# Chunked attention, then a two-layer leaky network: Q's copies on ScalarE, whole-tile exponentials, and a new written order

## The chip, the cores and the metric

The kernel runs on one core of one Trainium2 chip. The metric is the device time of one execution in microseconds (us), and the number compared is the median over several executions. The core's engines work side by side, each through its own list of instructions in order, and wait for each other through semaphores. The profile's names are: PE (TensorE matmuls), PEld (TensorE weight loads), DVE (VectorE), ACT (ScalarE), POOL (GpSimd) and SP (SyncE, here only a queue of DMAs).

## What is computed

Inputs are q, k and v of shape (8, 8, 576, 64), and two weight matrices of 512 x 2048 and 2048 x 512, all float32. The output is 4608 x 512, float32.

```python
q_c, k_c, v_c = (t.reshape(B, H, nc, 64, D) for t in (q, k, v))      # chunks of 64 positions
scores = q_c @ k_c.T / sqrt(D)
scores = scores - max(scores, axis=-1)
attn = exp(scores);  attn = attn / (sum(attn, axis=-1) + 1e-9)
out = attn @ v_c
x = out.transpose(0, 2, 1, 3).reshape(4608, 512)
h = x @ w_in
y = maximum(0.01 * h, h) @ w_out
```

## The kernel before

**Attention.** The tokens are cut into 36 units `u` of 128 positions (two chunks, all eight heads). For a unit, Q and K are loaded as 16-bit floats by POOL's DMA queue (`g`), and turned so that the head dimension lies on the partitions: for early units by TensorE transposes (`tq`, `tk`), from unit 14 on by transposing DMAs on SP's queue (`tdq`, `tdk`; lines 560 and 566), which land in tiles `QT` and `KT`. Q then goes into one of three standing tiles `QZ` whose other half is zero, by two copies of 64 partitions each (`cq`, line 573). `s` makes eight small matmuls, which give the scores `Sp` (one PSUM bank for all units) of 128 rows x 8 groups x 64.

**Softmax.** Two ways stand side by side. In the first, `m` takes the row maximum (line 591, DVE), `b` subtracts it from the whole score tile (line 596, DVE, in place in PSUM from unit 9 on), `x` makes one exponential of the whole tile (line 628, ACT), and `z` sums the rows (638), adds the tiny constant (640, tile `ze`) and takes the reciprocal (642), all on DVE. In the second, which the units 14, 16, 18, ... 34 use (eleven of the 36), `nb` multiplies the maximum by the negative scale (line 605, DVE, 128 x 8), and `f` makes eight exponentials of 64 columns each, with `nb` as bias, and lets ACT sum the rows on the way (line 613); `z` then leaves out its row sum. After either, `n` normalises (line 648; on POOL from unit 10 on), a transposing DMA turns the result (`d`, line 671, SP's queue), `v` multiplies with V, and `a` copies the attention output into `xT` on ACT (line 705).

**Network.** The tokens are worked in blocks `j`: two of 128 tokens, then 17 of 256. From block 2 on the second layer, and from block 9 on the first too, is done by seven half-size products in place of eight, which need sums and differences of the operands. First layer: `M` (line 321) up to block 8, with `G` (line 335, ACT) as leaky evacuation; from block 9 on `V` (line 418), with evacuations `lx` (ACT, line 449), `la` (DVE, line 455, adds a kept half) and `lp` (leaky, ACT, line 437), and sums `xs` of the input (line 389, POOL for most blocks). Second layer: `sum` makes the operand sums `SG` (line 205; the fourth of each of the blocks 8 to 15 is on POOL, the others on DVE), `R` the products (line 229), and `comb` the evacuations (ACT, lines 262 and 281, tiles `keep` and `osb`; DVE, line 283) and the store by SP's queue.

**What sets the order.** All of this is emitted by one written-out string, `ORDER`: a list of stage names with arguments, walked from left to right. Each stage issues its instructions at that point, so each engine's list, and SP's and POOL's queues, are in the order of the string. PSUM banks of the `m` kind are given out by a second string, `BANKS`, in the same walk. Nothing is reordered afterwards; a waiting instruction holds up all behind it on its engine.

```python
        nc.vector.tensor_copy(out=QZ[u % NQZ][part, :, :, s, :], in_=QT[u][part])           # stage_cq
        (nc.gpsimd if u >= UP else nc.vector).tensor_tensor(                                # stage_n
        (nc.gpsimd if (j, n) in SG_POOL else nc.vector).tensor_tensor(out=SG[j, n], in0=x, in1=y, op=op)
        (nc.gpsimd if j in XS_POOL else nc.vector).tensor_tensor(out=s[:, n - 1], in0=x, in1=y, op=op)
```

Of the kernel before, what the change touches and what calls it, by code (L numbers as in the profile page):

```python
# [8 lines left out]
FP16 = mybir.dt.float16  # L9
FP32 = mybir.dt.float32  # L10
# [6 lines left out]
def kernel(  # L17
# [52 lines left out]
    def need(*what):  # L70
        assert what in made, what
# [69 lines left out]
    minus = sbp.tile([128, 8], FP32, name="minus")  # L141
    nc.vector.memset(minus, -SCL)
# [427 lines left out]
    def stage_cq(u, s):  # L570
        made.add(("dq", u, s))
        part = slice(s * CH, (s + 1) * CH)
        nc.vector.tensor_copy(out=QZ[u % NQZ][part, :, :, s, :], in_=QT[u][part])
# [26 lines left out]
    Z: dict[int, bass.AP] = {}  # L600
    NB: dict[int, bass.AP] = {}

    def stage_nb(u):
        NB[u] = sbp.tile([128, 8], FP32, name="nb", tag="nb", bufs=2)
        nc.vector.tensor_tensor(out=NB[u], in0=MX.pop(u), in1=minus, op=ALU.mult)  # L605

    def stage_f(u, i0, i1):

        if i0 == 0:
            E[u] = sbp.tile([128, 8, CH], FP16, name="ex", tag="ex", bufs=2)  # L610
            Z[u] = sbp.tile([128, 8], FP32, name="z", tag="z", bufs=2)
        for i in range(i0, i1):
            nc.scalar.activation(  # L613
                out=E[u][:, i, :],
                in_=SP[u][:, i, :],
                func=AFT.Exp,
                bias=NB[u][:, i:i + 1],
                scale=SCL,
                accum_out=Z[u][:, i:i + 1],
            )  # L620
        made.add(("f", u, i0))
        if i1 == 8:
            need("f", u, 0)
            del SP[u], NB[u]

# [6 lines left out]
    def stage_z(u):  # L632
        if u in Z:
            need("f", u, 4)
            z = Z.pop(u)
        else:
            z = sbp.tile([128, 8], FP32, name="z", tag="z", bufs=2)
            nc.vector.tensor_reduce(out=z, in_=E[u], axis=AXL.X, op=ALU.add)
        ze = sbp.tile([128, 8], FP32, name="ze", tag="ze", bufs=2)
        nc.vector.tensor_tensor(out=ze, in0=z, in1=tiny, op=ALU.add)  # L640
        ZI[u] = sbp.tile([128, 8], FP32, name="zi", tag="zi", bufs=2)
        nc.vector.reciprocal(out=ZI[u], in_=ze)  # L642
# [107 lines left out]
    def zero_act(i):  # L750
# [151 lines left out]
```

## Time and profile before

| what | value |
|---|---|
| time, median of 3 runs | 281.63 us (279.67 to 282.55) |
| profiled execution, its own time | 281.67 us |
| span of the profile in that execution | 279.9 us |
| busy PE / PEld | 267.9 us / 243.7 us |
| busy DVE / ACT / POOL | 231.2 us / 202.3 us / 165.2 us |
| mean granted TensorE clock | 0.994 |

The span runs from the first instruction of the program to the last; the 1.8 us between it and the execution's own time lie outside the profile. Busy shares are averages over a start-up (about 18 us, until the first layer begins), a long middle part and a tail; what a wait costs is read where it stands.

### The profile page before, as it was taken

To read this page: it belongs to the slowest core of one execution; us is meant where nothing else is said; L and a number is where in the kernel's file an instruction comes from. 1 tells how busy PE (TensorE), PEld (TensorE's weight loads), DVE (VectorE), ACT (ScalarE), POOL (GpSimd) and SP (SyncE) were. 2 spreads that over 40 slices of the span, in tenths; PEclk is the share of its full clock that TensorE was granted. 3 is DMA by queue.
4 is the path that set the end of the run, shared out by engine and by line. 5 is a ranking of instruction groups with operands and counts; after the bars stand their busy time and mean duration, and the time that the engine had idled before them with its cause. 6 is when DMAs were issued, how large, how long until landed. Compare 5 with 4: busy or idle time off the path is not lost.

```text
span 279.9 us, 9161 instructions
## 1 busy us (share of the span) xinstructions
PE 267.9 (96%) x3705; PEld 243.7 (87%) x3705; DVE 231.2 (83%) x461; ACT 202.3 (72%) x531; POOL 165.2 (59%) x190
## 2 busy tenths in 40 slices
PE   7879999999999999999899897999999999999994
PEld 4569967999999999999898896999998999999994
DVE  7875679999987759888789999989999888587773
ACT  5656644675757775766797887989897997867661
POOL 8838646970374181968689666798979456003000
PEclk9979999999999999999999999999999999999999
DMA  9999999999699999999999969499999905020213
GB/s 149 139 187 183 206 178 156 155 145 125 115 131 159 206 187 200 139 165 164 200 101 201 165 124 105 115 132 127 175 178 151 158 15 115 4 94 2 78 40 112
DMA packets 159242, 38.35 MB, mean 137 GB/s; under 512 B 150240, under 2 KB 154720, under 8 KB 159200
## 3 DMA queue, kind: packets, MB, share of 16 engines
q0 software_dynamic: 111392, 18.10, 95.1%
q1 hardware_dynamic: 46768, 19.41, 37.5%
q8 instruction: 29, 0.48, 0.7%
q10 hardware_dynamic: 1040, 0.26, 0.4%
q14 instruction: 13, 0.11, 0.1%
HBM read 36.70 MB, written 9.44 MB: 165 GB/s over the span
## 4 chain that ended last, share of the span: by engine, by line
PE 74%; DVE 12%; ACT 4%; DMA 3%; POOL 3%; issue 2%; DVEq 0%; ACTq 0%; POOLq 0%
PE hT L321 19%; PE prX L229 17%; PE xbank L418 10%; PE xpr L418 7%; PE pr L229 6%; PE prZ L229 4%; DMA w_inT<-in_moe_w_in_dram 3%; DVE ze L640 3%; PE prW L229 2%; PE oP L464 2%; PE Sp L582 2%; PE xp L684 2%; DVE SG L205 2%; DVE xkeep L455 2%; ACT ex L613 2%
## 5 line engine op out<-in xcount | busy, mean ns | idle before, releaser
L321 PE MATMUL hT<-xT,w_inT 128*128 128x128 f16 (+1 forms) x768 | 63.7, 240 | 0.2 <-DMA w_inT<-in_moe_w_in_dram 0.2
L229 PEld LDWEIGHTS <-SG 128*128 128x128 f16 x544 | 51.0, 98 | 7.5 <-issue 1.9
L648 POOL TENSOR_TENSOR en<-ex,zi 128x512 f16<-128x512 f16 x26 | 28.0, 1077 | 49.9 <-DVE zi L642 15.9
L321 PEld LDWEIGHTS <-w_inT 128*128 128x128 f16 x768 | 54.7, 99 | 2.9 <-issue 0.2
L455 DVE TENSOR_TENSOR xkeep<-xpr,xkeep 128x512 f32<-128x512 f32 x60 | 39.3, 682 | 10.1 <-ACT xkeep L449 7.4
L335 ACT ACTIVATE gT<-hT 128x512 f16<-128x512 f32 x64 | 36.5, 603 | 11.4 <-PE hT L321 11.2
L449 ACT ACTIVATE xkeep<-xbank 128x512 f32<-128x512 f32 x60 | 36.1, 625 | 6.8 <-PE xbank L418 6.5
L229 PEld LDWEIGHTS <-gT 128*128 128x128 f16 x400 | 37.3, 98 | 4.3 <-ACT gT L437 0.3
L418 PEld LDWEIGHTS <-WS 128*128 128x128 f16 x640 | 38.2, 98 | 1.4 <-DVE xkeep L455 0.8
L437 ACT ACTIVATE gT<-xkeep 128x512 f16<-128x512 f32 x56 | 33.7, 661 | 6.2 <-DVE xkeep L455 6.2
L91 POOL DMA_DIRECT2D k_in<-in_k_dram x39 | 32.7, 841 | 9.0 <-DMA VB<-in_v_dram 5.3
L91 POOL DMA_DIRECT2D q_in<-in_q_dram x39 | 33.5, 865 | 5.6 <-DMA w_outT<-in_moe_w_out_dram 2.6
L229 PE MATMUL prX<-TW,SG 128*128 128x256 f16 x272 | 35.3, 273 | 0.2 <-DVE SG L205 0.2
L262 ACT ACTIVATE keep<-prX 128x256 f32<-128x256 f32 x51 | 20.4, 401 | 20.7 <-PE prX L229 19.3
L418 PEld LDWEIGHTS <-w_inT 128*128 128x128 f16 x480 | 29.1, 98 | 1.8 <-issue 1.1
L591 DVE TENSOR_REDUCE mx<-Sp 128x8 f32<-128x512 f32 x36 | 24.5, 682 | 6.5 <-PE Sp L582 6.0
L205 DVE TENSOR_TENSOR SG<-gT 128x1024 f16<-128x1024 f16 x34 | 24.5, 720 | 3.8 <-ACT gT L335 3.5
L613 ACT ACTIVATE ex<-Sp,nb 128x64 f16<-128x64 f32 x88 | 26.3, 331 | 1.8 <-DVE nb L605 1.7
L705 ACT ACTIVATE xT<-xp 128x512 f16<-128x512 f32 x36 | 22.2, 617 | 6.4 <-PE xp L684 6.3
L98 POOL DMA_DIRECT2D VB<-in_v_dram x24 | 23.3, 978 | 4.0 <-PE xp L684 4.0
L418 PE MATMUL xbank<-xs,WS 128*128 128x128 f16 x320 | 22.9, 219 | 0.0
L205 POOL TENSOR_TENSOR SG<-gT,SG 128x1024 f16<-128x1024 f16 x8 | 17.3, 2167 | 9.1 <-DVE SG L205 4.2
(96 smaller groups left out, 510.3 us busy)
## 6 DMA issues: line engine op xcount, KB each, us to landing
out_dram<-osb SPq DMA_DIRECT2D x35, 256.0 KB, 3.1
q_in<-in_q_dram POOLq DMA_DIRECT2D x31, 128.0 KB, 5.9
k_in<-in_k_dram POOLq DMA_DIRECT2D x31, 128.0 KB, 6.8
VB<-in_v_dram POOLq DMA_DIRECT2D x8, 288.0 KB, 7.4
VB<-in_v_dram POOLq DMA_DIRECT2D x16, 144.0 KB, 4.7
w_inT<-in_moe_w_in_dram POOLq DMA_DIRECT2D x8, 256.0 KB, 7.7
w_outT<-in_moe_w_out_dram POOLq DMA_DIRECT2D x4, 512.0 KB, 11.1
q_in<-in_q_dram POOLq DMA_DIRECT2D x8, 64.0 KB, 6.4
```

Of the source, the lines that this page charges most:

```text
L91: nc.gpsimd.dma_start(out=to, in_=rows)
L205: (nc.gpsimd if (j, n) in SG_POOL else nc.vector).tensor_tensor(out=SG[j, n], in0=x, in1=y, op=op)
L229: nc.tensor.matmul(out=to[:, i, :], lhsT=left[:, f, i * 128:(i + 1) * 128], rhs=right[:, f, :], start=(j, where) not in opened, stop=(f == ...
L321: nc.tensor.matmul(out=hT[:, i, :], lhsT=w_inT[:, t, fc * 128:(fc + 1) * 128], rhs=xT[:, t, r0:r0 + tb], start=(t == 0), stop=(t == NT - 1),)
L335: nc.scalar.activation(out=gT[j][:, nf * a:nf * a + nf, c0:c0 + tb], in_=HT.pop((j, a, p)), func=AFT.Prelu, bias=0.0, scale=1.0, alpha=0.01,)
L418: nc.tensor.matmul(out=to[:, i, :], lhsT=left[:, t, i * 128:(i + 1) * 128], rhs=right[:, t], start=(n in (1, 2, 5) and t == 0 and i == 0), ...
L437: nc.scalar.activation(out=gT[j][:, f0:f0 + 4, hi * 128:hi * 128 + 128], in_=of, func=AFT.Prelu, bias=0.0, scale=1.0, alpha=0.01)
L449: nc.scalar.activation(out=XK[j, s, n], in_=XB[j, s], func=AFT.Copy, bias=0.0, scale=1.0)
L455: nc.vector.tensor_tensor(out=to, in0=of, in1=to, op=ALU.add)
L591: nc.vector.tensor_reduce(out=MX[u], in_=SP[u], axis=AXL.X, op=ALU.max)
L613: nc.scalar.activation(out=E[u][:, i, :], in_=SP[u][:, i, :], func=AFT.Exp, bias=NB[u][:, i:i + 1], scale=SCL, accum_out=Z[u][:, i:i + 1],)
L648: (nc.gpsimd if u >= UP else nc.vector).tensor_tensor(out=E[u], in0=ex, in1=ZI.pop(u).unsqueeze(2).to_broadcast((128, 8, CH)), op=ALU.mult)
```

## The change

Three things are changed together.

1. `stage_cq` gets a flag, and all 44 copies of Q into `QZ` that take a transposed DMA's result now carry it: they are ACTIVATE copies on ACT, and no longer copies on DVE.
2. `nb` and `f` are gone. All 36 units take the maximum off with `b` on DVE, make one exponential of 128 x 512 with `x` on ACT, and sum the rows in `z` on DVE. A constant tile (`minus`) and its memset go with them.
3. `ORDER` is written anew from end to end. The stages and the products in it are the same apart from 1 and 2, and `BANKS`, `LOADS`, the number of filler matmuls and the assignment of sums to POOL stay.

```diff
-    minus = sbp.tile([128, 8], FP32, name="minus")
-    nc.vector.memset(minus, -SCL)
...
-    def stage_cq(u, s):
+    def stage_cq(u, s, act=0):
         made.add(("dq", u, s))
         part = slice(s * CH, (s + 1) * CH)
-        nc.vector.tensor_copy(out=QZ[u % NQZ][part, :, :, s, :], in_=QT[u][part])
+        to = QZ[u % NQZ][part, :, :, s, :]
+        if act:
+            nc.scalar.activation(out=to, in_=QT[u][part], func=AFT.Copy, bias=0.0, scale=1.0)
+        else:
+            nc.vector.tensor_copy(out=to, in_=QT[u][part])
...
-    def stage_nb(u):
-        NB[u] = sbp.tile([128, 8], FP32, name="nb", tag="nb", bufs=2)
-        nc.vector.tensor_tensor(out=NB[u], in0=MX.pop(u), in1=minus, op=ALU.mult)
...
-        for i in range(i0, i1):
-            nc.scalar.activation(
-                out=E[u][:, i, :],
-                in_=SP[u][:, i, :],
-                func=AFT.Exp,
-                bias=NB[u][:, i:i + 1],
-                scale=SCL,
-                accum_out=Z[u][:, i:i + 1],
-            )
...
     def stage_z(u):
-        if u in Z:
-            need("f", u, 4)
-            z = Z.pop(u)
-        else:
-            z = sbp.tile([128, 8], FP32, name="z", tag="z", bufs=2)
-            nc.vector.tensor_reduce(out=z, in_=E[u], axis=AXL.X, op=ALU.add)
+        z = sbp.tile([128, 8], FP32, name="z", tag="z", bufs=2)
+        nc.vector.tensor_reduce(out=z, in_=E[u], axis=AXL.X, op=ALU.add)
...
     ORDER = (
-        "R7.3.0 tdq23 d18 cq23.1 d19 tdk22 tdq24 f20.0.4 f20.4.8 z20 comb7.3 comb7.4 G8.6.0 G8.7.0 tdk23 G8.5.0 V9.0.1 "
...
-        "lx11.1.1 comb10.1 cq26.0 cq27.1 cq25.0 comb9.3 d23 sum10.2 z24 vl6.0 xs11.4 sum10.4 g30 n24 V11.0.2 V11.1.2 "
...
+        "d18 st640 tdk23 x20 cq22.1.1 G8.6.0 cq22.0.1 z20 comb7.3 comb7.4 G8.5.0 G8.7.0 cq23.1.1 st512 d19 V9.0.1 s21 "
...
+        "x24 tdk27 comb9.4 lp10.0.1.0 comb9.3 la10.1.3 z24 V11.0.1 V11.1.1 v22 s25 R10.1.0 lp10.1.1.1 lp10.1.1.0 "
+        "cq27.0.1 lx11.0.1 lx11.1.1 a22 comb10.1 sum10.2 vl6.0 sum10.4 g30 xs11.4 n24 V11.0.2 V11.1.2 R10.2.0 la11.0.2 "
```

Three places show what the new order does.

**VectorE at the entry of block 9**, where the unit 20 is in its softmax and the last sums of the block 7 are evacuated (`mx` the maximum, `Sp` the scores, `QZ` the tiles of Q, `osb` the output rows, `ze` and `zi` the row sum and its reciprocal, `SG` operand sums of the second layer). Before:

```order
L591 TENSOR_REDUCE mx<-Sp 128x8
L605 TENSOR_TENSOR nb<-mx,minus 128x8
L573 COPY QZ_66<-QT 64x8x64
L283 TENSOR_TENSOR osb_2722<-prZ,keep 128x256
L573 COPY QZ_67<-QT 64x8x64
L640 TENSOR_TENSOR ze<-z,tiny 128x8
L642 RECIPROCAL zi<-ze 128x8
L283 TENSOR_TENSOR osb_2618<-prZ,keep 128x256
L205 TENSOR_TENSOR SG<-gT 128x1024
```

And of the changed kernel, whose line numbers are lower by 2 to 28:

```order
L593 TENSOR_REDUCE mx<-Sp 128x8
L598 TENSOR_TENSOR Sp<-Sp,mx 128x512
L281 TENSOR_TENSOR osb_2697<-prZ,keep 128x256
L610 TENSOR_REDUCE z<-ex 128x8
L612 TENSOR_TENSOR ze<-z,tiny 128x8
L614 RECIPROCAL zi<-ze 128x8
L281 TENSOR_TENSOR osb_2634<-prZ,keep 128x256
L203 TENSOR_TENSOR SG<-gT 128x1024
```

The multiplication `nb` and two copies have left this stretch; a subtraction over the whole tile and a row sum have come in.

**ScalarE at the same place**, from the exponentials of the unit 20 to the first evacuations of the block 9 (`gT` the hidden layer, `xkeep` a kept quarter of the first layer). Before:

```order
L613 ACTIVATE ex,z<-Sp,nb 128x64 x8
L281 ACTIVATE osb_2722<-prX 128x256
L335 ACTIVATE gT<-hT 128x512 x3
L449 ACTIVATE xkeep<-xbank 128x512 x2
L262 ACTIVATE keep<-prX 128x256
```

And of the changed kernel:

```order
L604 ACTIVATE ex<-Sp 128x512
L573 ACTIVATE QZ_66<-QT 64x8x64
L333 ACTIVATE gT<-hT 128x512
L573 ACTIVATE QZ_66<-QT 64x8x64
L279 ACTIVATE osb_2697<-prX 128x256
L333 ACTIVATE gT<-hT 128x512 x2
L573 ACTIVATE QZ_67<-QT 64x8x64
L573 ACTIVATE QZ_65<-QT 64x8x64
L447 ACTIVATE xkeep<-xbank 128x512
```

Eight exponentials became one, and four copies of Q, for the units 22, 23 and 24, stand between the evacuations.

**VectorE around the row sum of the unit 24**, where the block 10's second layer begins. POOL's fourth sum of the block 10 waits for the second of the two `SG` rows. Before:

```order
L283 TENSOR_TENSOR osb_3252<-prZ,keep 128x256
L205 TENSOR_TENSOR SG<-gT 128x1024
L205 TENSOR_TENSOR SG<-SG,gT 128x1024
L640 TENSOR_TENSOR ze<-z,tiny 128x8
L642 RECIPROCAL zi<-ze 128x8
L455 TENSOR_TENSOR xkeep<-xpr,xkeep 128x512
L591 TENSOR_REDUCE mx<-Sp 128x8
```

And of the changed kernel:

```order
L453 TENSOR_TENSOR xkeep<-xpr,xkeep 128x512
L610 TENSOR_REDUCE z<-ex 128x8
L612 TENSOR_TENSOR ze<-z,tiny 128x8
L614 RECIPROCAL zi<-ze 128x8
L203 TENSOR_TENSOR SG<-gT 128x1024
L203 TENSOR_TENSOR SG<-SG,gT 128x1024
L453 TENSOR_TENSOR xkeep<-xpr,xkeep 128x512 x2
```

The addition `ze` stood behind the two sums and now stands ahead of them.

More of the change, by code (lines that the diff above doesn't have):

```diff
@@ L598, in stage_b @@
         )
-    Z: dict[int, bass.AP] = {}
-    NB: dict[int, bass.AP] = {}
-    def stage_nb(u):
-        NB[u] = sbp.tile([128, 8], FP32, name="nb", tag="nb", bufs=2)
[L605 to L611, printed above, removed]
-        for i in range(i0, i1):
-            nc.scalar.activation(
-                out=E[u][:, i, :],
-                in_=SP[u][:, i, :],
-                func=AFT.Exp,
-                bias=NB[u][:, i:i + 1],
-                scale=SCL,
-                accum_out=Z[u][:, i:i + 1],
-            )
[L621 to L624, printed above, removed]
     def stage_x(u):
@@ L853 @@
         "A": first_layer, "H": first_act, "S": first_sum, "G": act1, "B": second_layer, "O": finish, "i": idle, "y": zero, "w": zero_act,
-        "I": identity, "st": store_held, "nb": stage_nb, "f": stage_f, "tdk": stage_tdk, "tdq": stage_tdq, "cq": stage_cq,
+        "I": identity, "st": store_held, "tdk": stage_tdk, "tdq": stage_tdq, "cq": stage_cq,
         "WS": w_in_sum, "vl": load_v_piece, "xs": x_sums, "lx": wide_x, "la": wide_m, "lp": leaky_kept,
```

164 rows, old and new, of the table ORDER are left out of this document.

## The prediction

> **What bounds the kernel now.** I read the page first, then the chain, then the stretches of 10 us, and last the instructions around the holes on PE. The rows from the page are the span, the busy times and the shares of the chain that ended last.
>
> ```profile
> span 279.9 us, 9161 instructions
> PE 267.9 (96%) x3705; PEld 243.7 (87%) x3705; DVE 231.2 (83%) x461; ACT 202.3 (72%) x531; POOL 165.2 (59%) x190
> PE 74%; DVE 12%; ACT 4%; DMA 3%; POOL 3%; issue 2%; DVEq 0%; ACTq 0%; POOLq 0%
> ```
>
> PE is busy 96% of the span and holds three quarters of the chain; DVE is the only other engine with a share worth asking about. So the question is where PE has holes. The stretches (columns: the stretch, its length, then busy time and instruction count of PE, PEld, DVE, ACT and POOL, granted clock, DMA share, GB/s) tell it:
>
> ```profile
> 10.00:20.00 10.00, 7.34 (x121) 5.41 (x117) 8.25 (x18) 5.87 (x10) 4.84 (x9) 0.91 1.59 166
> 20.00:30.00 10.00, 10.00 (x180) 10.00 (x179) 4.34 (x10) 6.05 (x12) 8.59 (x11) 0.92 1.49 187
> ...
> 130.00:140.00 10.00, 9.22 (x120) 8.49 (x119) 7.30 (x15) 6.58 (x26) 7.34 (x9) 1.00 1.95 179
> ...
> 150.00:160.00 10.00, 8.76 (x133) 8.12 (x131) 9.40 (x15) 7.35 (x21) 7.83 (x9) 1.00 1.94 191
> 160.00:170.00 10.00, 9.00 (x126) 8.34 (x124) 9.71 (x17) 7.66 (x26) 7.31 (x8) 1.00 0.73 123
> 170.00:180.00 10.00, 9.46 (x148) 8.56 (x146) 9.52 (x22) 9.46 (x32) 6.18 (x9) 1.00 0.71 105
> 180.00:190.00 10.00, 10.00 (x151) 9.53 (x149) 8.73 (x18) 8.98 (x30) 9.92 (x12) 1.00 1.62 137
> 190.00:200.00 10.00, 10.00 (x160) 9.53 (x158) 9.48 (x22) 9.39 (x23) 8.98 (x10) 1.00 1.49 164
> 200.00:210.00 10.00, 10.00 (x146) 9.48 (x144) 9.33 (x19) 9.40 (x31) 8.23 (x9) 1.00 1.28 154
> 210.00:220.00 10.00, 9.80 (x151) 9.03 (x149) 9.66 (x20) 8.45 (x29) 8.11 (x11) 1.00 2.11 145
> 220.00:230.00 10.00, 9.96 (x149) 9.26 (x147) 8.37 (x17) 9.94 (x33) 6.03 (x7) 1.00 0.27 81
> ```
>
> After the start-up PE is idle only in six of these stretches: 0.78 + 1.24 + 1.00 + 0.54 + 0.20 + 0.04 = 3.8 us. A hole costs a little more than its idle time, because a group of eight matmuls is shown busy for 1.04 us while the next group can start 0.87 us after it:
>
> ```profile
> 139.15 1.04 PE L229 MATMUL prX<-TW,SG 128*128 128x256 f16 x8
> 140.02 1.04 PE L229 MATMUL prZ<-TW,SG 128*128 128x256 f16 x8
> ```
>
> So 0.17 us more per hole. PE's waits after the start-up are seven, the four of the rows below and three of 0.2 to 0.5 us, so about 3.8 + 1.2 = 5.0 us of the span are lost in the middle. That is the most that any edit which leaves the matmuls as they are can win there: 281.7 - 5.0 = 276.7 us. Who is waited for, in total, count and longest:
>
> ```profile
> PE prZ L229 <- DVE xkeep L455: 1.6, 2, 1.0
> PE xbank L418 <- ACT gT L335: 0.8, 1, 0.8
> PE Sp L582 <- ACT ex L628: 0.7, 1, 0.7
> ```
>
> DVE and ACT evacuate too late there. Why they are late shows in the order of time, where DVE's instructions stand beside POOL's:
>
> ```profile
> 129.06 2.27 DVE L605 TENSOR_TENSOR nb<-mx,minus 128x8 f32<-128x8 f32 x1
> 129.00 1.06 POOL L648 TENSOR_TENSOR en<-ex,zi 128x512 f16<-128x512 f16 x1
> 130.01 1.29 POOL L389 TENSOR_TENSOR xs<-xT 128x256 f16<-128x256 f16 x2
> ...
> 150.33 2.79 DVE L640 TENSOR_TENSOR ze<-z,tiny 128x8 f32<-128x8 f32 x1 [0.47 <-ACT ex L613]
> 150.35 2.11 POOL L205 TENSOR_TENSOR SG<-gT,SG 128x1024 f16<-128x1024 f16 x1
> ...
> 165.19 3.21 DVE L640 TENSOR_TENSOR ze<-z,tiny 128x8 f32<-128x8 f32 x1
> 166.26 2.12 POOL L205 TENSOR_TENSOR SG<-gT,SG 128x1024 f16<-128x1024 f16 x1
> ...
> 212.09 1.56 DVE L205 TENSOR_TENSOR SG<-gT 128x1024 f16<-128x1024 f16 x1
> ```
>
> An operation on 128 x 8 numbers takes 2.3 to 3.2 us, and ends just when POOL's run of tensor operations ends. DVE is held while POOL computes. Each stretch with holes has such a hold in it or just ahead of it: 130:140 the first row, 150:160 the `ze` at 150.33, 160:180 the `ze` at 165.19, 210:220 the held sum. **The limit is PE, with 5 us lost to an evacuation path that DVE's holds push past it.**
>
> **The change part by part.** The groups that it touches (busy us, mean ns of one, idle before):
>
> ```profile
> L573 DVE COPY QZ<-QT 64x512 f16<-64x512 f16 x44 | 18.8, 427 | 2.4 <-DMA QT<-q_in 1.7
> L605 DVE TENSOR_TENSOR nb<-mx,minus 128x8 f32<-128x8 f32 x11 | 5.2, 470 | 0.3
> L596 DVE TENSOR_TENSOR Sp<-Sp,mx 128x512 f32<-128x512 f32 x16 | 11.1, 694 | 0.5
> L638 DVE TENSOR_REDUCE z<-ex 128x8 f32<-128x512 f16 x25 | 16.8, 674 | 3.1 <-ACT ex L628 2.9
> L640 DVE TENSOR_TENSOR ze<-z,tiny 128x8 f32<-128x8 f32 x36 | 13.3, 369 | 1.9 <-ACT ex L613 1.0
> L541 ACT ACTIVATE QZ<-qp 64x512 f16<-64x512 f16 x7 | 5.0, 710 | 1.2 <-PE qp L519 1.2
> ...
> 24.92 0.59 ACT L541 ACTIVATE QZ<-qp 64x512 f16<-64x512 f16 x1
> 128.04 1.08 ACT L335 ACTIVATE gT<-hT 128x512 f16<-128x512 f32 x2 [0.85 <-PE hT L321]
> 146.89 1.18 ACT ex L613 x8
> ```
>
> And three answers for a line alone in a stretch of 50 us (busy time and count): line 613, exponentials and read-outs together, then line 573, the copies, then line 640, `ze`.
>
> ```profile
> 180.00:230.00 50.00, 10.04 (x64) 1.00 1.35 136
> 180.00:230.00 50.00, 6.20 (x14) 1.00 1.35 136
> 130.00:180.00 50.00, 6.83 (x7) 1.00 1.41 144
> ```
>
> *DVE.* Out go 44 copies (18.8 us) and 11 multiplications (5.2 us), in come 11 subtractions of 0.69 us (7.6 us) and 11 row sums of 0.67 us (7.4 us): -24.0 + 15.0 = -9.0 us of 231.2. The seven `ze` of 130:180 took 6.83 us, two of them 6.0, so one that isn't held takes under 0.2; were the copies and multiplications never held, the exchange would bring DVE next to nothing. What it wins is held time. For the unit itself the way gets no longer: a multiplication and 2.36 us of exponentials against 0.69 + 0.48 + 0.67 = 1.84 us, on two engines instead of one, and the score bank is free about 1.2 us earlier (0.69 + 0.48 against 2.36).
>
> *ACT.* A unit's eight exponentials are two halves of 1.18 us (four exponentials with their read-outs), 2.36 us; one exponential takes its place at the pace of a 512-wide ACTIVATE, of which two in a row end 1.08 us after the start where one takes 0.60, so 0.48 us each. Eleven times 1.88 is 20.7 us out. The copies of 64 x 512 come in. No row shows ACT copying them from SBUF. The nearest is the one at 24.92, of the same shape and with whole rows of 64 contiguous numbers: 0.59 us long, so 0.48 at pace; the dear end is the mean of all seven, 0.71, of which six write scattered numbers. I take 0.48: 44 x 0.48 = 21.1 us in, and **ACT stays where it is (+0.4 us)**; at 0.71 it would be 31.2 us in and ACT +10.5. ACT is fullest in 180:230, where its five rows add up to 46.2 of 50 us. There it loses 64 instructions, that is four units' exponentials (-10.0), for four wide ones (+1.9) and gains about 14 copies (+6.7 or +9.9): 44.8 to 48.0 of 50, covered by PE's 50 either way. If that cover were gone, each us over 50 would be a us of span.
>
> The Trainium skill's page "ScalarE: Activation LUTs", section "What ACT_TABLE_LOAD costs", speaks a little against the move: an ACTIVATE with immediate bias is 186 ns plus 0.833 ns an element whatever the partitions, with 93 ns overlapped, which gives 0.52 us for such a copy as an estimate from that page, and ACT +2.2 us in place of +0.4, where the row at 24.92 has 0.59 us for a length that the page puts at 0.61. The end by it is the same 278.8, as ACT is covered.
>
> *What is moved.* The list of stages is the same, so SP's and POOL's queues carry the same transfers and the same POOL operations; they meet others. At the entry of block 9 `nb` is gone: its 2.27 us, for which the exponentials of unit 20 and behind them the evacuation `gT` and PE's `xbank` waited, cannot come back, since the subtraction that replaces it reads the scores from PSUM like the 16 rows of 0.694 mean that show no hold. That is the hole in 130:140: 0.78 + 0.17 = **0.95 us won**. At the entry of block 10's second layer the `ze` of unit 24 now stands ahead of the two sums for whose second POOL's long sum waits, so POOL cannot be in that sum: the holes in 160:180 (1.00 + 0.54, two of them, 1.54 + 0.34 = **1.9 us**) lose their cause. The `ze` of unit 22, which the hole in 150:160 follows, still stands right behind the block 9's two sums, with POOL's `xs` sums about it; I leave that hole (1.24 + 0.34) and the small ones of 210:230 as they are, 2.1 us. The start-up's matmuls, fillers and weight loads keep their order but for small swaps, and it ends on a weight transfer; I count it at nothing. If that cover were gone it would be by the clock: 0.91 and 0.92 granted in the first two rows of the stretches are 0.9 + 0.8 = 1.7 us, which could be won or paid once more.
>
> The Trainium skill's page "TensorE: Matmul & The Clock Gate", section "What's actually happening", has that gate look at a free-running window of 3.4 us, so that the same program may lose more or less. The two rows agree in size, and the sum by it is the same with 1.7 us to either side.
>
> **The sum:** 281.67 - 0.95 - 1.88 = **278.8 us**. It is made against the profiled execution, 281.67, which agrees with the median 281.63. A measurement of this kernel tells no change apart from one of 1%, about 2.8 us.
>
> **The rivals.**
>
> *All holes close: 276.7.* For it: DVE loses 9 us where it was fullest (9.4 to 9.7 of 10 in 150:180), so a remaining hold may fall into slack. Against it: 36 `ze` and the `SG` rows stay on DVE, POOL's busy time is unchanged. Chance 0.16.
>
> *The holds only move: about 281.5.* `ze` was held 2.79 and 3.21 us in two of seven cases of 130:180, both times under POOL's sum of 2.1 us; in a new order another two can meet POOL's long sums, for example `ze` of the units 22, 23 or 31, which stand near the fourth sums of the blocks 9 and 13. Each such meeting opened 1.6 (1.24 + 0.34) to 1.9 us of holes. One or two of them take back 1.6 to 3.5 of the gain: 280.4 to 282.3. Against it: in five of the six blocks 10 to 15 the new list has a `ze` ahead of the sums, not behind. Chance 0.22. The Trainium skill's page "SBUF — State Buffer", section "SBUF: two separate sides", has DVE and POOL share one port pair by an exclusive lock, held for a whole instruction by whichever came first, and counts operations with two SBUF inputs among those locked out. By that rule every `ze` stays exposed however few copies are left, and the rows above agree.
>
> *ACT takes over the wait for Q's transposing DMA: 284.8, slower.* On DVE the copies waited for `QT`, and DVE's queue absorbed it:
>
> ```profile
> DVE QZ L573 <- DMA QT<-q_in: 1.7, 2, 1.0
> ```
>
> On ACT the same wait holds up `gT`, `xkeep` and `xT` behind it, and a late `gT` of about that size cost PE 0.95 us. The place: the copies of the units 21 and 23, listed closest behind their transposes, the latter just ahead of block 9's first `xkeep`. Three such waits of 1.0 us, the longest seen, eat the 2.8 us won; from six on it is slower by over 1%, 278.8 + 6 x 1.0 = 284.8. Against it: only two waits in 44 were seen, and the new list has several evacuations between transpose and copy. Chance 0.17.
>
> That the change doesn't do what it says isn't open: the lists show 44 copies on ACT and no `nb`.
>
> **How the numbers follow.** The forecast, 277.8 to 280.0 with its unknowns, has 0.45; the rivals 0.16, 0.22 and 0.17. Faster by over 1% is below 278.8: the first rival and half of the forecast, 0.39. Slower by over 1% is above 284.4: the last rival and a little of the second, 0.18. Within 1% is the rest, 0.43. The range takes in the first rival less 0.4 for a start-up that loses less to the clock, the second rival with 1.7 us of clock paid again (282.3 + 1.7 = 284.0), and leaves out the last from six waits on: 276.3 to 284.2.
>
> **What the changed profile would show.** Right: DVE about 222 us busy, ACT within 2 us of 202; copies on ACT near 0.6 us long; no DVE instruction longer than 2 us in 125:140 and 160:175; PE idle in 120:230 near 1.6 us in place of 3.8. Wrong: `ze` or `SG` rows over 2 us with holes on PE behind them (second rival); ACT rows waiting for `QT`, with evacuations behind (third); PE idle in 30:120, where it had none, since there the new order has everything to lose.

## The result, and the profile after

The changed kernel takes 279.75 us (median of 16 runs, 278.26 to 283.79) against 281.44 us for the kernel before, run beside it: ratio **0.9945, interval 0.992 to 0.9971**. It is faster by 0.55%, a real gain but within the 1% that the prediction called no change. This ratio and those below leave disturbed executions out, so a ratio can differ a little from that of the medians. The forecast was 278.8 us, 0.9 us too low, inside its range.

The profiled execution took 278.98 us, 2.69 less than the one before. Rows of its page:

```profile
span 277.2 us, 9023 instructions
PE 266.6 (96%) x3705; PEld 243.2 (88%) x3705; DVE 220.9 (80%) x427; ACT 208.1 (75%) x410; POOL 164.3 (59%) x190
PE 81%; DMA 7%; ACT 6%; DVE 4%; issue 1%; SPq 0%; ACTq 0%
```

DVE lost 10.3 us, ACT gained 5.8, and PE is as full as it was. The chain tells more: DVE's share fell from 12% to 4%, POOL's 3% is gone, and DMA's rose from 3% to 7%. The stretches of 10 us (columns as in the prediction; those of 30 to 240 us that are not shown have PE at 10.00):

```profile
10.00:20.00 10.00, 8.49 (x154) 6.54 (x152) 9.03 (x19) 7.15 (x12) 5.71 (x10) 1.00 1.73 179
20.00:30.00 10.00, 10.00 (x195) 10.00 (x193) 7.27 (x14) 7.81 (x16) 9.11 (x11) 1.00 1.46 197
...
60.00:70.00 10.00, 9.23 (x133) 8.46 (x132) 7.90 (x19) 4.67 (x11) 1.17 (x2) 1.00 1.66 162
90.00:100.00 10.00, 8.58 (x91) 7.65 (x90) 7.01 (x11) 5.83 (x12) 3.98 (x4) 1.00 2.00 141
130.00:140.00 10.00, 9.79 (x126) 8.86 (x124) 6.22 (x13) 7.08 (x14) 5.02 (x5) 1.00 1.40 195
140.00:150.00 10.00, 9.52 (x144) 8.94 (x143) 8.16 (x16) 9.48 (x20) 9.92 (x13) 1.00 2.03 115
150.00:160.00 10.00, 9.74 (x147) 9.16 (x145) 7.54 (x17) 9.04 (x19) 8.62 (x10) 1.00 1.79 180
160.00:170.00 10.00, 10.00 (x154) 9.53 (x152) 9.51 (x18) 9.76 (x21) 7.19 (x8) 1.00 1.87 154
170.00:180.00 10.00, 10.00 (x161) 9.55 (x157) 9.19 (x19) 9.09 (x20) 8.61 (x12) 1.00 1.09 146
190.00:200.00 10.00, 9.58 (x139) 8.97 (x138) 8.70 (x17) 9.88 (x21) 9.70 (x10) 1.00 1.75 171
```

Between 120 and 230 us PE idles 0.21 + 0.48 + 0.26 + 0.42 = 1.4 us where it idled 3.8. Between 30 and 120, where it had no hole, it now idles 0.77 + 1.42 = 2.2. With 0.17 us more for each hole, six before and six now, 4.8 us lost became 4.6.

Where the 2.69 us went can be read from the starts of the same products. The first product of the first layer (`hT`) starts at 17.64 us in place of 18.42, which is 0.8. From there to the start of PE's last product it is 255.8 us in place of 257.7, which is 1.9. Of this the clock explains 1.1 to 1.7: the first two rows are granted 1.00 where they had 0.91 and 0.92, a stretch of 3.4 us at 0.50 from 18.17 us on, so 1.7 at most. The old order without one addition (below), which had the full clock there, takes 113.8 us from the first `hT` to the first `xbank` product where the kernel before took 114.9; this gives the 1.1. So 0.2 to 0.8 us are left for the middle. The medians, in which start-up and clock vary on both sides, give 1.7 us.

Who PE waits for now (total, count, longest):

```profile
PE xp L656 <- DMA et<-en: 2.2, 2, 1.4
...
PE xbank L416 <- ACT xkeep L447: 1.2, 3, 0.5
...
PE prZ L227 <- DVE xkeep L453: 0.2, 1, 0.2
```

After the start-up, DVE as the one waited for has shrunk to 0.2 us. In its place stand the transposing DMA of `et` and ACT's evacuations. First the DMA, in PE's order of time:

```profile
60.57 1.04 PE L227 MATMUL prX<-TW,SG 128*128 128x256 f16 x8
62.37 0.39 PE L656 MATMUL xp<-et,VB 128*128 128x64 f16 x8 [0.77 <-DMA et<-en]
...
95.28 0.40 PE L584 MATMUL Sp<-KT,QZ 128*128 128x64 f16 x8
97.10 0.39 PE L656 MATMUL xp<-et,VB 128*128 128x64 f16 x8 [1.42 <-DMA et<-en]
```

The time from issue to landing for the two transposes around 54 to 59 us, and for the two around 87 to 95 us, min, median and max, the kernel before ahead of the changed one each time. Before:

```profile
DMA to landing us min/median/max: 6.7/6.8/7.0
DMA to landing us min/median/max: 5.8/6.6/7.5
```

After:

```profile
DMA to landing us min/median/max: 7.3/7.7/8.0
DMA to landing us min/median/max: 7.4/8.9/10.4
```

The transposes take 0.3 to 3 us longer. In the kernel before, the `xp` of unit 6 began 1.6 us after its data were there and that of unit 12 also 1.6; now both begin the moment the data land. For unit 6 the margin is used up from both sides: PE comes to its `xp` 7.3 us after the issue where it was 8.3, and the transfer takes 8.0 us in place of 6.7. For unit 12 PE comes after 9.0 us as before, and the transfer alone has grown, from 7.5 to 10.4. Over all the profiles of this case the transfer of unit 12 took 7.5 to 8.0 us in the old order and 9.0 to 10.4 in the new one; for unit 6 the two ranges overlap (6.3 to 7.9 and 6.7 to 8.3).

Then ACT, whose queue in the hole at 158.0 us reads:

```profile
156.32 0.63 ACT L435 ACTIVATE gT<-xkeep 128x512 f16<-128x512 f32 x1
156.98 0.63 ACT L573 ACTIVATE QZ<-QT 64x512 f16<-64x512 f16 x1
157.63 1.08 ACT L447 ACTIVATE xkeep<-xbank 128x512 f32<-128x512 f32 x2
```

A copy stands directly ahead of the evacuation that PE's `xbank` waits for; the same picture is at 197 us. At 144 us four evacuations stand between, but ACT's queue has no gap from the copy at 142.10 on. The group of the copies, and line 612, `ze`, alone in 130:180:

```profile
L573 ACT ACTIVATE QZ<-QT 64x512 f16<-64x512 f16 x44 | 27.3, 626 | 1.0 <-PE prX L227 0.4
130.00:180.00 50.00, 1.75 (x7) 1.00 1.64 158
162.99 0.68 DVE L610 TENSOR_REDUCE z<-ex 128x8 f32<-128x512 f16 x1
163.70 0.17 DVE L612 TENSOR_TENSOR ze<-z,tiny 128x8 f32<-128x8 f32 x1
164.09 0.67 DVE L203 TENSOR_TENSOR SG<-gT 128x1024 f16<-128x1024 f16 x1
...
209.96 1.22 DVE L612 TENSOR_TENSOR ze<-z,tiny 128x8 f32<-128x8 f32 x1
```

ACT never waited for `QT`. The seven `ze` that took 6.83 us take 1.75. The next three rows are DVE at the entry of block 10's second layer: the `ze` that took 3.21 us behind the two sums takes 0.17 ahead of them. The last is the longest `ze` left.

### The profile page after: what moved, and what is told of

It reads as the page before. It is cut to its first block, busy times and chain, and to the rows that moved or that the text cites. A ratio compares the mean times of both kernels' runs of the same rounds, so it can differ in the third digit from the quotient of the medians.

```text
span 277.2 us, 9023 instructions
## 1 busy us (share of the span) xinstructions
PE 266.6 (96%) x3705; PEld 243.2 (88%) x3705; DVE 220.9 (80%) x427; ACT 208.1 (75%) x410; POOL 164.3 (59%) x190
## 4 chain that ended last, share of the span: by engine, by line
PE 81%; DMA 7%; ACT 6%; DVE 4%; issue 1%; SPq 0%; ACTq 0%
PE prX L227 19%; PE hT L319 16%; PE xbank L416 11%; PE xpr L416 9%; DMA et<-en 7%; PE prZ L227 6%; PE pr L227 5%; PE xp L656 3%; PE prW L227 3%; PE Sp L584 3%; PE oP L462 2%; PE idle L686 2%; ACT xkeep L447 2%; ACT xT L677 1%; ACT QZ L573 1%
## 5 line engine op out<-in xcount | busy, mean ns | idle before, releaser
L319 PE MATMUL hT<-xT,w_inT 128*128 128x128 f16 (+1 forms) x768 | 62.4, 237 | 0.0
L319 PEld LDWEIGHTS <-w_inT 128*128 128x128 f16 x768 | 53.5, 98 | 2.7
L447 ACT ACTIVATE xkeep<-xbank 128x512 f32<-128x512 f32 x60 | 34.3, 595 | 7.6 <-PE xbank L416 7.2
L260 ACT ACTIVATE keep<-prX 128x256 f32<-128x256 f32 x51 | 19.6, 384 | 18.6 <-PE prX L227 18.3
L435 ACT ACTIVATE gT<-xkeep 128x512 f16<-128x512 f32 x56 | 32.8, 627 | 0.7 <-DVE xkeep L453 0.6
L610 DVE TENSOR_REDUCE z<-ex 128x8 f32<-128x512 f16 x36 | 24.3, 675 | 6.9 <-ACT ex L604 6.7
L416 PEld LDWEIGHTS <-w_inT 128*128 128x128 f16 x480 | 29.1, 98 | 0.7
L573 ACT ACTIVATE QZ<-QT 64x512 f16<-64x512 f16 x44 | 27.3, 626 | 1.0 <-PE prX L227 0.4
L203 DVE TENSOR_TENSOR SG<-gT 128x1024 f16<-128x1024 f16 x34 | 25.3, 743 | 3.4 <-ACT gT L333 2.0
L677 ACT ACTIVATE xT<-xp 128x512 f16<-128x512 f32 x36 | 21.4, 595 | 5.6 <-PE xp L656 5.5
```

What stands on the lines that cost most here:

```text
L319: nc.tensor.matmul(out=hT[:, i, :], lhsT=w_inT[:, t, fc * 128:(fc + 1) * 128], rhs=xT[:, t, r0:r0 + tb], start=(t == 0), stop=(t == NT - 1),)
L416: nc.tensor.matmul(out=to[:, i, :], lhsT=left[:, t, i * 128:(i + 1) * 128], rhs=right[:, t], start=(n in (1, 2, 5) and t == 0 and i == 0), ...
L435: nc.scalar.activation(out=gT[j][:, f0:f0 + 4, hi * 128:hi * 128 + 128], in_=of, func=AFT.Prelu, bias=0.0, scale=1.0, alpha=0.01)
L447: nc.scalar.activation(out=XK[j, s, n], in_=XB[j, s], func=AFT.Copy, bias=0.0, scale=1.0)
L573: nc.scalar.activation(out=to, in_=QT[u][part], func=AFT.Copy, bias=0.0, scale=1.0)
```

## The experiments

Three theories stood at the start. **H**: what cost time was VectorE's `ze`, held under GpSimd's sums. **O**: the two parts of the change are worth something only in an order laid out for them. **D**: the part of the forecast that did not come went into the two waits for the transposing DMA. Each time is a median, with its ratio to the kernel before on the same chip. Where the text turns a ratio into us, it is the ratio times 281 us.

**Both parts in the old order.** The order list of before, with `nb` replaced by `b`, the two halves `f` by one `x`, and every copy on ACT.

```diff
-        nc.vector.tensor_copy(out=QZ[u % NQZ][part, :, :, s, :], in_=QT[u][part])
+        nc.scalar.activation(out=QZ[u % NQZ][part, :, :, s, :], in_=QT[u][part], func=AFT.Copy, bias=0.0, scale=1.0)
...
-        "... z13 sum5.1 m14 nb14 cq15.1 sum5.2 ... G6.0.0 f14.0.4 n13 R5.2.0 f14.4.8 ..."
+        "... z13 sum5.1 m14 b14 cq15.1 sum5.2 ... G6.0.0 x14 n13 R5.2.0 ..."
```

> The kernel before with parts 1 and 2 of the change alone: its written order stays, each nb is replaced by the subtraction b at the same place, the first half of f by the whole exponential x, the second half is left out, and all 44 copies of Q go to ACT. Theory H (holds: the holes on PE come from DVE being held under POOL's tensor operations, so fewer exposed DVE instructions are what pays): DVE near 222 us busy, the hole of 130:140 closed, part of the holes of 150:180 left because ze stays where it was; 280.0 to 281.0, ratio 0.994 to 0.998. Theory O (the new order is what pays, the two parts in an order laid out for other durations bring nothing): 281.4 to 283.5, ratio 1.000 to 1.007, with ACT's copies ahead of evacuations opening new holes.

288.04 us, ratio 1.0232 (1.0171 to 1.0294). The same two edits that come with a gain in the new order cost 6.5 us in the old one, more than either theory had expected. ACT's and PE's rows in order of time at the largest hole:

```profile
133.83 0.63 ACT L573 ACTIVATE QZ<-QT 64x512 f16<-64x512 f16 x1 [3.39 <-DMA QT<-q_in]
134.48 0.60 ACT L628 ACTIVATE ex<-Sp 128x512 f16<-128x512 f32 x1
134.98 0.38 ACT L281 ACTIVATE osb<-prX 128x256 f32<-128x256 f32 x1
135.24 1.58 ACT L335 ACTIVATE gT<-hT 128x512 f16<-128x512 f32 x3
...
135.90 0.61 PE L418 MATMUL xbank<-xT,w_inT 128*128 128x128 f16 x8 [2.38 <-ACT gT L335]
```

This is the prediction's third rival, in the other order: a copy waits for its transposing DMA, and the evacuation behind it comes 3.4 us late. PE idles 2.4 us, and the granted clock is 0.50 for the 3.4 us from 136.6 us on, which is up to 1.7 more. So this place explains up to 4.1 of the 6.5 us.

**Two weighted sums later.** The changed kernel, with the weighted sum `v` of units 6 and 12 listed two products later.

```diff
-  "... R3.2.0 R3.6.0 v6 sum3.3 ... R3.5.0 g11 tq11 R3.7.0 g12 ..."
+  "... R3.2.0 R3.6.0 sum3.3 ... R3.5.0 g11 tq11 R3.7.0 v6 g12 ..."
-  "... comb5.1 v12 R5.6.0 M6.3.0 M6.4.0 ..."
+  "... comb5.1 R5.6.0 M6.3.0 v12 M6.4.0 ..."
```

> The changed kernel, with two stages later in its order and nothing else: the multiplication with V of unit 6 behind the fifth and seventh product of block 3, that of unit 12 behind the sixth product of block 5 and one group of first-layer matmuls. Theory D (what the forecast lacks went into two waits of xp for a transposing DMA, 0.8 and 1.4 us of idle PE at 61 and 95 us, 2.5 us with what the pipeline loses): both waits go, nothing else moves, and the time falls by 2.0 to 2.5 us: about 277.4, ratio to the kernel before 0.984 to 0.988. Rival (the waits are cover for something else that is late there anyway, the scores or the evacuations behind): the wait comes back on the next instruction of PE and the time falls by less than 0.8 us: ratio 0.992 to 0.9945.

279.64 us, ratio 0.9952 (0.9919 to 0.9985): nothing won. The waits moved to the next units, 7 and 13, at 65 and 101 us, and an evacuation `keep` on ACT came late at 185.

**Without the addition.** Kernel before and changed kernel, each with the reciprocal taken of the row sum itself. What is left out is the addition of 1e-9 to a sum that is at least 1.

```diff
-        ze = sbp.tile([128, 8], FP32, name="ze", tag="ze", bufs=2)
-        nc.vector.tensor_tensor(out=ze, in0=z, in1=tiny, op=ALU.add)
...
-        nc.vector.reciprocal(out=ZI[u], in_=ze)
+        nc.vector.reciprocal(out=ZI[u], in_=z)
```

> The kernel before, without the addition of the tiny constant (tile ze) in any unit: the reciprocal is taken of the row sum itself, which is at least 1, so the constant is below the last digit of it in float32. 36 instructions leave DVE, 13.3 us of busy time, of which about 7.5 us were holds under POOL. Theory H: the holes of 150:160 and 160:180 (1.6 and 1.9 us) go, as their ze did; 278.0 to 279.3, ratio 0.988 to 0.9925. Rival (ze was only the instruction that happened to wait; the next one with two SBUF inputs, or the evacuations that ACT is late with, take its place): less than 1 us, ratio 0.996 to 1.000.

> The changed kernel, with the same addition left out (36 instructions, 9.5 us of DVE's busy time, of which about 3.7 us are holds, none over 1.1 us). Theory H: since no hole of the changed kernel stands behind a long hold of ze, the time stays within 0.5 us: ratio to the kernel before 0.993 to 0.9965, and the two waits for the transposing DMA at 61 and 95 us stay. Rival (DVE's busy time as such, not single long holds, is what counts): 9.5 us less of it gives 1 us or more: below 0.991.

The kernel before goes to **275.48 us, ratio 0.9818 (0.9765 to 0.9871)**, three times the gain of the change and more than theory H had expected. The changed kernel stays: 279.45 us, 0.9936 (0.9904 to 0.9967). Page and stretches of the former:

```profile
span 272.6 us, 9122 instructions
PE 265.6 (97%) x3705; PEld 242.1 (89%) x3705; DVE 220.0 (81%) x425; ACT 202.7 (74%) x531; POOL 165.0 (61%) x190
...
130.00:140.00 10.00, 10.00 (x151) 9.50 (x149) 8.36 (x16) 7.32 (x18) 7.47 (x8) 1.00 2.00 174
150.00:160.00 10.00, 10.00 (x154) 9.53 (x153) 9.15 (x20) 9.13 (x30) 6.65 (x9) 1.00 2.14 197
160.00:170.00 10.00, 10.00 (x156) 9.54 (x154) 8.38 (x18) 8.83 (x31) 9.75 (x11) 1.00 1.78 117
170.00:180.00 10.00, 9.96 (x156) 9.23 (x154) 8.43 (x17) 9.51 (x24) 8.58 (x10) 1.00 1.22 149
```

All holes of the old order are gone, with all 44 copies on DVE and all eleven `nb` in place, and though an `nb` was still held 1.68 us at 125.88 and a copy 1.73 us at 83. DVE's load is 220.0 us, just that of the changed kernel. From the first `xbank` product to PE's last one it is 137.8 us where the kernel before took 142.8: the 5.0 us are the holes. So in the old order the lever was `ze`: its going does all that the moved copies were to do.

**Each part alone in the old order.** One subtraction and one exponential, copies left on DVE; then the copies on ACT, exponentials left as they were. The edits are the two halves of the first diff.

> The kernel before with the eleven units changed to one subtraction and one exponential, the copies left on VectorE and the order list otherwise as before. Theory H (only ze held under GpSimd's long sums costs time; the holds of nb cost nothing): the two long ze holds stay, so about 281.4 us, between 280.5 and 283; VectorE gains 11 x (0.70 + 0.68) = 15 us of work and loses eleven nb, ScalarE loses 11 x 1.88 = 21 us. Theory P (my prediction's second step: nb held before the 130:140 hole is a cause): the hole at 133.7 goes, 0.95 us, so about 280.5. Theory O (parts in an order laid out for other durations cost): at 284 or more, about half of the 6.6 us of both parts together.

> The kernel before with all 44 copies into QZ on ScalarE, the eleven units' eight exponentials and the order list as before. If the 6.6 us that both parts cost in the old order come from the copies (ScalarE's queue waits for the transposing DMA of QT with evacuations behind the copy), nearly all of them are here: 286 to 289 us, with ScalarE's L573 waiting over 2 us for DMA QT and PE waiting for gT in 130:140. If they come from the exponentials' part, about 281.5. ScalarE has 21 us more work than with both parts, so a time over 289 would say that its load matters beside its order.

The exponentials alone: 283.5 us, 1.0059 (1.0022 to 1.0096). The copies alone: 293.91 us, **1.0439 (1.0391 to 1.0488)**. In the first, DVE at the place where `nb` had been held:

```profile
130.35 0.70 DVE L596 TENSOR_TENSOR Sp<-Sp,mx 128x512 f32<-128x512 f32 x1
131.08 1.68 DVE L573 COPY QZ<-QT 64x512 f16<-64x512 f16 x1
132.79 0.42 DVE L283 TENSOR_TENSOR osb<-prZ,keep 128x256 f32<-128x256 f32 x1
```

The subtraction is not held, as the prediction said, but the copy behind it is: GpSimd's run of operations still stands there. PE's hole at that place shrank and did not close (0.37 us idle after 0.78). Theory P, that removing `nb` wins this hole by itself, falls. The `ze` held before the hole of 150:160 stays (2.64 us at 151.02), and so do the holes behind it. In the second, ACT's 228.3 us leave no room; the two late stretches, with PE's, DVE's and ACT's busy time and the granted clock:

```profile
130.00:180.00 50.00, 43.13 (x601) 39.52 (x600) 35.40 (x61) 42.86 (x123) 33.83 (x37) 0.97 1.28 130
180.00:230.00 50.00, 44.28 (x621) 40.33 (x618) 34.69 (x68) 46.35 (x140) 36.41 (x41) 0.97 1.18 130
```

PE idles 12.6 us there, and every wait of over 1 us after the start-up is for ACT. The time lies over the 286 to 289 us expected from ACT's order alone, which by the expectation says that its load counts as well; ACT waited for `QT` once, 1.7 us. Both parts together (6.5 us) are dearer than the exponentials alone (1.7) and cheaper than the copies alone (12.3), so the exponentials pay back about half of what the copies cost; they take 20 us off ACT.

**The copies back on DVE, in the new order.** 
```diff
-        if act:
+        if False:
             nc.scalar.activation(out=to, in_=QT[u][part], func=AFT.Copy, bias=0.0, scale=1.0)
```

> The changed kernel with its 44 copies back on VectorE, in the new order. VectorE gets 44 x 0.47 = 21 us more (to about 242), ScalarE 27 us less. If the copies' place is worth nothing in itself and the order brought the gain: 279 to 280.5 us, and the waits for ScalarE's xkeep at 144, 158 and 197 (1.6 us) are gone while some for VectorE come. If relieving VectorE is what brought the gain: 281.5 to 284, with ze or the copies held over 1.5 us and PE waiting for VectorE's evacuations.

290.49 us, 1.0269 (1.0202 to 1.0335). PE's longest waits:

```profile
PE Sp L584 <- DVE QZ L575: 2.4, 2, 2.2
PE xpr L416 <- DVE xkeep L453: 1.6, 1, 1.6
```

Both expectations were too low. The new order needs the copies on ACT much as the old one needs them on DVE: putting them on the other engine costs 9.1 us here (1.0269 against 0.9945) and 12.3 there. The move has no worth of its own apart from the order it stands in.

**One `ze` earlier in the old order.**

```diff
-  "... comb9.3 d23 sum10.2 z24 vl6.0 ..."
+  "... comb9.3 d23 z24 sum10.2 vl6.0 ..."
```

> The kernel before with one entry of the order list moved: the sum and ze of unit 24 ahead of GpSimd's token sum of 10.2 instead of behind it. Theory H, and the third step of the prediction: the ze held 3.2 us at 165 us is free, the holes of PE at 168 and 170 (1.17 and 0.66 us) go and nothing else changes: 279.5 us, between 279 and 280.3. If the hole only comes later (sum 10.2 or the next evacuation late instead): 281 to 282.

280.35 us, ratio 0.9962 (0.9926 to 0.9997): about 1.1 us, and anything from 0.1 to 2.1 by the interval, where the prediction gave these holes 1.9. DVE there:

```profile
167.50 0.67 DVE L640 TENSOR_TENSOR ze<-z,tiny 128x8 f32<-128x8 f32 x1 [1.19 <-ACT ex L613]
...
168.75 0.64 DVE L205 TENSOR_TENSOR SG<-gT 128x1024 f16<-128x1024 f16 x1
```

The hold of 3.21 us is gone, but `ze` now stands where its row sums are not yet there: ACT's eight exponentials keep DVE waiting 1.19 us, and the sums behind are late. PE's hole at 169 became a wait for `SG` of 0.9 us. In the profiled execution PE idles 1.45 us in 160:180 where it idled 1.54, so there the holes only changed their cause.

**Repairs of the new order.** First four weighted sums later (units 6, 7, 12, 13); then eight of the 44 copies behind the evacuations they stood ahead of; then both; then both without the addition, which leaves out what the runs without it above left out.

```diff
-  "... R3.6.0 v6 sum3.3 ... R3.3.0 comb3.7 ... R3.4.0 v7 tk11 comb3.4 a7 k11 s10 M4.0.1 M4.1.1 m10 ..."
+  "... R3.6.0 sum3.3 ... R3.3.0 v6 comb3.7 ... R3.4.0 tk11 comb3.4 k11 s10 M4.0.1 M4.1.1 v7 a7 m10 ..."
-  "... comb5.1 v12 R5.6.0 M6.3.0 M6.4.0 ... M6.6.0 v13 R5.4.0 ... M6.7.0 b16 ..."
+  "... comb5.1 R5.6.0 M6.3.0 M6.4.0 v12 ... M6.6.0 R5.4.0 ... M6.7.0 v13 b16 ..."
...
-  "... V9.1.2 cq24.1.1 lx9.0.1 comb8.1 lx9.1.1 sum8.2 ..."
+  "... V9.1.2 lx9.0.1 comb8.1 lx9.1.1 cq24.1.1 sum8.2 ..."
```

> The changed kernel with the weighted sums of units 6, 7, 12 and 13 all moved behind later products (with two of them moved the wait had come back on the other two). If the waits of xp for the transposing DMA at 61 and 95 us (0.93 and 1.59 us) are time on TensorE's path: about 277.3 us, 276.8 to 278, ratio to the kernel before 0.985, and no wait of xp for DMA et left before 130 us. If something else fills the place (the next unit's DMA, or ScalarE late later on): 279 to 280, with the holes listed further on growing.

> The changed kernel with eight of its 44 copies put on ScalarE behind the evacuations of xbank that they stood in front of (units 24, 26, 27, 28, 30, 31 twice and 33); the weighted sums stay as in the changed kernel. If the holes at 144, 158 and 197 us (0.64, 0.42 and 0.58 us) are the copy's 0.63 us in front of the evacuation: they go, about 278.2 us, ratio 0.989. If the evacuation is late for another reason: 279.7, holes as before. If a copy is now late for its scores: over 281, with PE waiting for L573.

> Both repairs of the changed kernel's order: four weighted sums later, eight copies behind the evacuations. If both groups of waits are independent holes of TensorE: about 275.7 us, 275 to 276.7, ratio 0.980, which would be the floor of 276.7 us that the prediction gave for no holes after the start-up, less its clock window. If removed waits come back elsewhere: 278 to 280.

> The changed kernel's order with both repairs, and without the addition of 1e-9 to the row sums (which are at least 1, so that the addition is below their last digit). Theory H: in this order ze is held nowhere over 1.3 us, so its leaving is worth nothing, with or without the waits for the DMA: 277 us, 276.3 to 277.8, ratio 0.988. If VectorE's load itself still costs time once the other holes are gone: 275 to 276, about that of the kernel before without the addition (ratio 0.982).

| kernel | us | ratio to before | interval |
|---|---|---|---|
| four weighted sums later | 278.31 | 0.9911 | 0.9879 to 0.9944 |
| eight copies behind | 279.14 | 0.9949 | 0.9917 to 0.998 |
| both | 277.06 | 0.9891 | 0.9844 to 0.9938 |
| both, without the addition | 277.04 | 0.988 | 0.983 to 0.993 |

With four moved, no wait of `xp` for the DMA is left, and by the ratio about 1 us of the 2.2 is won, as theory D would have it for that half. A new hole of 0.75 us idle stands at 184, a wait for ACT's `keep`. Moving the copies closed the holes at 144 and 197 but opened one of 0.85 us at 170, again for `keep`, so alone it wins nothing. The first three times each lie between the two that had been expected. Each interval overlaps that of the changed kernel; only their order, and the waits, speak for the sums. The last row fits H: in the new order no cost of the addition is seen, with the DMA's waits all but gone, though the intervals would hide one of up to about 2 us. PE's waits in it:

```profile
PE prX L227 <- ACT keep L260: 0.6, 1, 0.6
...
PE xbank L416 <- ACT xkeep L447: 0.3, 1, 0.3
PE xp L654 <- DMA et<-en: 0.3, 1, 0.3
```

What is left there is mostly waiting for ACT. The fastest kernel by its median is the one before without the addition, 275.48 us; its interval overlaps that of the kernel with both repairs.

## Why the prediction was right, and where it wasn't

**What bounds the kernel: right, and the limit holds.** PE sets the end, 5.0 us were lost in holes, and the kernel of 275.48 us has hardly one. (The prediction counted seven waits; six lie behind the start-up, which makes 4.8 us, but the starts of the products give 5.0 as well.) That lies 1.2 us below the 276.7 given for no holes; the floor was taken from an execution that had lost 1.1 to 1.7 us to the clock in the start-up, which this kernel's profiled execution did not pay.

**DVE, -9.0 us: right** (-10.3, to 220.9; 222 was said).

**ACT, +0.4 us: mis-sized.** The term was the copy: 0.48 us, the length of the row at 24.92 less an overlap seen on evacuations. Measured are 0.626 us each; from one start to the next it is 0.65 in the rows at 156 us, and 0.54 where the next instruction overlaps (142.10 to 142.64 us). So 27.3 us came in rather than 21.1, and ACT gained 5.8. The Trainium skill's page "ScalarE: Activation LUTs", section "What ACT_TABLE_LOAD costs", gives 0.61 us for such an operation, near the measured length, but with its 93 ns overlapped 0.52, and that overlap the trace shows behind about half of the copies. ACT in 180:230 is 46.50 of 50 us, within the 44.8 to 48.0 given, but the step that followed, "covered by PE's 50 either way", was wrong: busy time below 50 did not keep PE from idling 0.3 to 0.5 us, three times between 140 and 200 us, for an evacuation that stood behind copies.

**The hole at 130:140 (0.95 us won): the effect came, the cause was too narrow.** PE idles 0.21 us there and no DVE operation is held. But with `nb` alone removed the copy behind it was held instead. It took the copies' leaving DVE as well, or, in the old order, the missing addition.

**The holes of 160:180 (1.9 us won): right.** Both rows are at 10.00, and the `ze` ahead of the sums takes 0.17 us. Moved alone in the old order it won about 1.1 (0.1 to 2.1), and there it had to wait for ACT's row sums; in the new kernel they come from DVE's own reduction just ahead (162.99 to 163.67), and nothing waits.

**The hole of 150:160, said to stay: wrong.** The `ze` of unit 22, held 2.79 us before, takes 0.23, and GpSimd's long sum now starts behind it:

```profile
150.75 0.23 DVE L612 TENSOR_TENSOR ze<-z,tiny 128x8 f32<-128x8 f32 x1
...
152.42 2.13 POOL L203 TENSOR_TENSOR SG<-gT,SG 128x1024 f16<-128x1024 f16 x1
```

So 1.24 us closed that were not forecast, and the small holes of 210:230 with them, while ACT's late `xkeep` opened 0.48 in 140:150, 0.26 in 150:160 and 0.42 in 190:200. That 120:230 idles 1.4 us where 1.6 was forecast is luck: two errors cancel.

**What failed: the step "The list of stages is the same, so SP's and POOL's queues carry the same transfers ... they meet others", costed at nothing.** The prediction named the sign, PE idle in 30:120, without giving it a price or a place. There the weighted sums of units 6 and 12 had 1.6 us of margin before, and the new order has none: 2.2 us idle, 2.5 lost. That eats most of what 120:230 gave: the middle won 0.2 to 0.8 us in place of 2.8. That the profiled execution, 278.98 us, still comes out beside 278.8 is luck as well: the start-up (0.8, counted at nothing) and the clock (1.1 to 1.7, not in the sum) gave the rest. The medians, with 1.7 us, say that the change is worth a little more than the middle alone; the starts of the first `hT`, 17.3 to 20.8 us in the profiles of the old order and 17.6 to 20.1 in those of the new one, do not tell whether the start-up is part of it.

**The rivals.** All holes closed: no, though the old order without one small addition reached it. Holds only move: no, the longest left in `ze` is 1.22 us, with no hole behind it; so the rule of the Trainium skill's page "SBUF — State Buffer", section "SBUF: two separate sides", that a hold threatens each `ze`, is borne out as a risk and not as a price, since the price hangs on what GpSimd does at that moment. ACT taking over the wait for `QT`: not in the new order, but in the old one, where one such wait with the clock behind it was up to 4.1 of the 6.5 us lost. That rival was sound in mechanism. That the new list kept it away by putting more work between transpose and copy fits its rows, since `QT` took up to 10.2 us to land and no copy waited for it, but was not tried alone.

**What stays open.** How much of the 5.1 us that the missing addition wins in the old order is holds, and how much the 11 us less work on DVE; that the same removal wins nothing in the new order speaks for holds, but there DVE is less loaded too. Why the transpose of unit 12 takes longer in the new order was not tried, nor was the start-up.

## What to carry to other kernels

Moving work between engines and rewriting the order are one edit: here the copies cost 9 to 12 us on the engine for which the order was not made, and the pair of them won 1.7. When a tiny operation on VectorE takes microseconds, look at what GpSimd runs beside it, and first ask whether the operation is needed at all. After a new order, compare the margin between each transfer's landing and its use with that of before, in the stretches that had no holes too: a place without a hole is not a place with slack.

## What the runs showed of the hardware

An addition of 128 x 8 numbers took 0.17 us alone and up to 3.21 us beside GpSimd's tensor operations; a subtraction with PSUM on its input, at the same place, 0.70 us and no more.

Long waits of PE went with a lower granted clock. After the start-up, and but for the last few us, the changed kernel's rows and those of the kernel without the addition have a granted clock of 1.00, while the kernel with the copies alone on ACT has 0.97 in both late stretches of 50 us. Each of the two is one stretch of 3.41 us at half the clock:

```profile
136.08:139.49 3.41, 3.41 (x32) 3.05 (x31) 2.90 (x6) 1.41 (x4) 2.15 (x2) 0.50 0.63 184
214.59:218.00 3.41, 3.12 (x30) 2.58 (x30) 2.36 (x6) 3.41 (x9) 0.00 (x0) 0.50 1.35 247
```

That is up to 1.7 us lost each, beside 12.6 us of idle time in all. In the 3.41 us just ahead of them PE was busy 1.29 and 1.53 us; behind 1.75 us, from 170.21 us on, no such stretch followed. In the start-up of the kernel before one followed 1.82 us (14.76 to 18.17 us), so the busy time alone does not settle it. The Trainium skill's page "TensorE: Matmul & The Clock Gate", section "What's actually happening", has the gate look at windows of 3.4 us; as an estimate from that page, one such window at half speed loses 1.7 us, and the rows agree.
